# Sliding-window attention and a squared-ReLU feed-forward on one core: Strassen in seven up-projections instead of five, k and q of the short blocks in one transpose, and a scheduler's order shifted by fixed draws

## The chip, the cores and the metric

The kernel runs on one core of a Trainium2 chip. A core has five engines with a queue each: TensorE (PE, with its weight loads shown apart as PEld), VectorE (DVE), ScalarE (ACT), GpSimd (POOL) and SyncE (SP). Here PE does all matmuls and some transposes, DVE and ACT move and transform what PE leaves in its accumulation memory (PSUM, eight banks of 128 x 512 floats), POOL issues the input transfers, SP issues the output transfers and the transposes that the DMA engines do. The metric is the time on the device of one execution, in microseconds. The time before is the median of three runs, 292.88 (292.44 to 293.42).

## The reference

Eight batches, eight heads, 576 tokens, head size 64. Each token attends to itself and the 127 tokens before it, with a linear bias by distance whose slope depends on the head. The result, as 4608 tokens of 512 features, goes through a feed-forward of width 2048 with a squared ReLU.

```python
scores = scale * np.matmul(q, k.transpose(0, 1, 3, 2))
mask = (rel >= 0) & (rel < window)
scores = np.where(mask, scores + bias[None], -1000000000.0)
attn = np.exp(scores)  # after the row maximum is taken off
attn = attn / (np.sum(attn, axis=-1, keepdims=True) + 1e-09)
x = np.matmul(attn, v)              # then (batch, token, head*feature)
h = x @ w_in
r = np.maximum(h, 0.0)
return ((r * r) @ w_out).astype(np.float32)
```

## The kernel before

**Blocks and groups.** Attention works on blocks of tokens: each batch of 576 tokens is four blocks of 128 and a last one of 64, so there are 40 blocks (numbered m), eight of them short (m = 4, 9, 14, ...). The feed-forward works on nine groups of 512 tokens (g = 0 to 8), which do not line up with the blocks. Inputs are cast to bf16 as they are loaded; accumulation is in float32.

**Attention of a block.** `load_block` has POOL load k, q and v of a block (line 423). k and q lie one behind the other in a tile `kq` of 128 x 2 x 512. `prepare` turns them so that features lie on partitions, into `kqT`: blocks 0 to 10 by eight PE transposes of 128 x 128 (line 473) and a copy out of PSUM; from block 11 on (`KQ_DMA`) by one DMA transpose issued by SP (line 453). In a short block the transpose turns all 128 rows, though only 64 carry tokens. `scores` multiplies q with the keys of the block and of the one before it (lines 523 and 542; short blocks and first blocks of a batch use the second), ACT takes the exponential (line 581), and DVE multiplies with a mask that holds bias and window (line 592, tile `P`). `values` multiplies P with v and a column of ones (line 622), DVE takes reciprocals and normalises (lines 645 and 655) into `x`, and x is turned into `xT` (features on partitions) by PE (line 681) up to block 12 and by a DMA transpose (line 669) from block 13 on. `xT` is a ring of four groups.

**Up-projection.** A plain group (`fc_step`, line 728) takes, for each of 16 slices of 128 hidden features, four matmuls of 512 columns; ACT applies the ReLU (line 741), and DVE or ACT squares (lines 749 and 751) into `g`. A group in `FAST` takes Strassen's algorithm instead, in Winograd's form with seven products of half-size blocks: `token_sums` builds three sums and differences of the tokens' quarters on DVE (line 771), and four calls of `fast_unit` each run seven products of four matmuls of 256 columns (line 802) in three PSUM banks. Between the products ACT copies banks into SBUF (`fs`, `fu`, `fx`; lines 862, 883 and 872), DVE adds one back into a bank (line 868) and adds two others while it reads a bank (line 836). ReLU is on ACT (line 830) or on DVE or ACT (lines 841 and 843), squares on DVE or ACT (lines 851 and 853). `FAST` holds groups 4 to 8. The products of weights need sums of quarters of `w_in`, built once by DVE in `weight_sums` (line 386): sixteen steps of two instructions each.

**Down-projection.** Group 0 is plain (line 1036); groups 1 to 8 use Strassen (line 957), 112 matmuls of 256 columns each, with sums of `g` on DVE (line 916).

**Order.** All work is a list of tasks with a key, dependencies, buffers, and one duration for each engine that can do it. `Plan.order` walks a model of the chip ahead of the launch: at each step it gives the engine that can start first the ready task with the least key (within a wait of 100 ns on DVE and ACT), picks DVE or ACT where both are possible, and hands out PSUM banks. The resulting order of instructions is fixed on each engine; on the chip, semaphores enforce the dependencies. A stage of the feed-forward spans 128 units of the key: in stage g the up-projection of group g + 1 and the down-projection of group g are interleaved, and blocks of attention get due keys ahead of the group that needs them. The argument `shift` of `order` adds an offset to the key of each named set of tasks (same function, same rounded key); before the change nobody passes it. The DMA costs given to `load` are numbers for this model.

Of the kernel before, what the change touches and what calls it, by code (L numbers as in the profile page):

```python
# [10 lines left out]
AF = mybir.ActivationFunctionType  # L11
# [189 lines left out]
def kernel(  # L201
    ctx: ExitStack, tc: tile.TileContext, q, k, v, moe_w_in, moe_w_out, out
):
    nc = tc.nc

    B, H, S, D = q.shape
# [21 lines left out]
    SQUARES = 352.0  # L228
    FAST = range(NG - 5, NG)
    RING = 4 * 512  # L230
# [40 lines left out]
    def act(n):  # L271
        return n * 0.836 + 50.0

    def dve(n, rate=1):
        return n / rate / 0.96 + 68.0
# [116 lines left out]
    def load_block(m, key):  # L392
# [4 lines left out]
        for i, (nm, src) in enumerate((("k", k), ("q", q), ("v", v))):  # L397
# [26 lines left out]
            t_in[m, nm] = load(key + 0.01 * i, 920.0 if n == 128 else 600.0, emit, [t_ones] + (t_zeros if m >= NKB - 1 else []) if nm == "v" else [], [sl])  # L424

# [15 lines left out]
    def prepare(m):  # L441
# [9 lines left out]
        if kq_by_dma:  # L451
            def turn_kq():
                nc.sync.dma_start_transpose(kqT[sk.idx], kq[s_in[m, "k"].idx].rearrange("s t f -> s (t f)"))
            t_kq = [plan.add({"SP": 2000.0}, due - 80, turn_kq, [t_in[m, "k"], t_in[m, "q"]], [sk],
                             [s_in[m, "k"]], dma=900.0)]
        else:
# [3 lines left out]
            shared = Slot("t")  # L460
            for j, nm in ((j, nm) for hf in range(C // step) for j, nm in enumerate("kq")):
                hf = len(t_kq) // 2
# [3 lines left out]
                for i in range(hf * step, hf * step + step):  # L466
# [3 lines left out]
                    def emit(i=i, j=j, nm=nm, slot=slot, opens=fresh and i == hf * step, alloc=alloc):  # L470
                        if opens and slot.tile is None:
# [4 lines left out]
                    last = plan.add({"PE": mm(128)}, due - 56 + hf, emit,  # L476
                                    [last, t_ident, t_in[m, nm][hf] if m == 0 else t_in[m, nm]] + (chain["tp"] if opens else []),
                                    ([slot] if fresh and opens else []) + ([sk] if opens and not t_kq else []),
                                    [s_in[m, nm]] if j == 1 and i == C - 1 else [])
# [3 lines left out]
                if not apart and j == 0:  # L483
                    t_kq.append(None)
                    continue

                def evac(k=len(t_kq), j=j, slot=slot, lo=hf * step, hi=hf * step + step):
                    if apart:
                        copy(t_kq[k], kqT[sk.idx][:, j * C + lo:j * C + hi, 0:n],
                             slot.tile[:, j * 512:(j + 1) * 512].rearrange("p (c s) -> p c s", c=C)[:, lo:hi, 0:n])  # L490
                    else:
                        copy(t_kq[k], kqT[sk.idx][:, :, 0:n],
                             slot.tile.rearrange("p (c s) -> p c s", c=2 * C)[:, :, 0:n])
                w = step * n * (1 if apart else 2)
                t_kq.append(plan.add({"ACT": act(w), "DVE": dve(w, 2)}, due - 56 + hf, evac, [last], [], [slot]))
# [9 lines left out]
    def scores(ms):  # L505
# [20 lines left out]
        def burst(cs=range(C)):  # L526
# [4 lines left out]
            for m, sk, n, kb, parts, squares, slots, sE in todo:  # L531
                own, prev = kqT[sk.idx], kqT[sk_of[m - 1].idx] if kb else None
                for c in cs:
# [3 lines left out]
                    for i, (part, mk) in enumerate(() if squares else parts):  # L537
                        for half in range(2):
# [3 lines left out]
                            nc.tensor.matmul(sl.tile[:, at:at + n], kqT[sk_of[mk].idx][rows, c, :],  # L542
                                             own[rows, C + c, 0:n], start=True, stop=True)
        deps, acq, rel, cost = list(chain["s"]), [], [], 216.0
# [17 lines left out]
        for m, sk, n, kb, parts, squares, slots, sE in todo:  # L562
# [9 lines left out]
            for i, sl in enumerate(slots):  # L572
                w = one * H // len(slots)

                def expo(sl=sl, i=i, w=w, scores_e=scores_e, one=one, whole=len(slots) == 4):
                    if whole:
# [4 lines left out]
                    nc.scalar.activation(o, src, AF.Exp, bias=0.0, scale=scale)  # L581
                te = plan.add({"ACT": act(w)}, due - 28 + 3 * i, expo, [halves[i // 2 if m == 0 else 0]], [], [sl])
                if squares and i < 2:
# [110 lines left out]
    m = 0  # L694
# [385 lines left out]

    done = plan.order()
    kernel.plan = done
# [46 lines left out]
```

## Time and profile before

| what | us |
|---|---|
| median of three runs | 292.88 |
| the profiled execution's own time | 294.55 |
| span of the profiled execution, first to last instruction | 292.8 |
| TensorE busy | 281.9 (96% of the span) |
| DVE busy | 241.8 (83%) |
| ACT busy | 223.2 (76%) |
| POOL busy | 105.7 (36%) |

The granted TensorE clock is 0.999 over the span. Busy times are unions of the records of an engine: a record may begin before the one before it has ended, so the mean duration of one instruction times the count is more than the time that they keep the engine. PE's records are of modelled length, and a few are missing.

### The profile page before, as it was taken

What the parts mean: (1) busy time and instruction counts of PE and PEld (TensorE: products, weight loads), DVE (VectorE), ACT (ScalarE), POOL (GpSimd) and SP (SyncE); (2) the same over time, 40 slices, a digit from 0 to 9 for tenths busy, and PEclk for the clock granted to TensorE, in tenths of its full rate; (3) what the DMA queues carried; (4) which work ended last, traced back from release to release, by engine and by line L of the source; (5) the groups of instructions that cost most, each with busy time, mean ns of one, the idle gap of its engine ahead of it and who ended that gap; (6) DMA issues with size and microseconds to landing.
All of it is one profiled execution on the core that took longest, in us unless ns stands there. A gap on an engine that the chain in (4) does not pass through costs nothing.

```text
span 292.8 us, 9190 instructions
## 1 busy us (share of the span) xinstructions
PE 281.9 (96%) x3756; PEld 230.0 (79%) x3777; DVE 241.8 (83%) x584; ACT 223.2 (76%) x438; POOL 105.7 (36%) x131
## 2 busy tenths in 40 slices
PE   7799799999999999999999999999999999999995
PEld 6689678875666676666878888888888888888884
DVE  6948878695989856776989899999999997989833
ACT  6648868985578947779698989989989789578520
POOL 8937777651906443743623364332000000000000
PEclk9999999999999999999999999999999999999999
DMA  9999999999999999999999999999423111301223
GB/s 136 172 189 163 162 185 173 151 164 201 149 154 129 150 164 198 169 172 144 202 179 146 162 159 185 131 143 189 74 74 108 37 30 39 107 2 36 75 72 107
DMA packets 169946, 39.40 MB, mean 135 GB/s; under 512 B 157104, under 2 KB 169392, under 8 KB 169904
## 3 DMA queue, kind: packets, MB, share of 16 engines
q0 software_dynamic: 114656, 18.10, 92.9%
q1 hardware_dynamic: 54192, 20.46, 38.0%
q8 instruction: 29, 0.48, 0.7%
q10 hardware_dynamic: 1056, 0.26, 0.4%
q14 instruction: 13, 0.11, 0.1%
HBM read 36.70 MB, written 9.44 MB: 158 GB/s over the span
## 4 chain that ended last, share of the span: by engine, by line
PE 83%; DMA 6%; DVE 5%; ACT 3%; issue 2%; POOL 0%; ACTq 0%
PE o L957 32%; PE f L802 19%; PE h L728 16%; PE pv L622 6%; DMA w_in_sb<-in_moe_w_in_dram 5%; PE o L1036 4%; PE ps_s L523 3%; DMA raw<-in_q_dram 1%; PE ps_s L542 1%; PE tp L473 1%; DVE rt L836 1%; PE xp L681 1%; ACT rt L741 1%; DVE P L592 1%; DVE g L851 1%
## 5 line engine op out<-in xcount | busy, mean ns | idle before, releaser
L728 PE MATMUL h<-xT,w_in_sb 128*128 128x128 bf16 (+2 forms) x499 | 67.4, 270 | 3.5 <-issue 2.2
L581 ACT ACTIVATE E<-ps_s 128x384 bf16<-128x384 f32 (+2 forms) x130 | 58.5, 517 | 7.8 <-PE ps_s L523 7.5
L423 POOL DMA_DIRECT2D vt<-in_v_dram x40 | 34.2, 856 | 67.0 <-PE pv L622 57.1
L957 PEld LDWEIGHTS <-g 128*128 128x128 bf16 x512 | 49.1, 98 | 9.0
L592 DVE TENSOR_TENSOR P<-E,masks 128x1024 bf16<-128x1024 bf16 (+1 forms) x67 | 43.6, 661 | 11.1 <-ACT E L581 10.6
L741 ACT ACTIVATE rt<-h 128x512 bf16<-128x512 f32 x64 | 37.8, 603 | 19.1 <-PE h L728 16.8
L728 PEld LDWEIGHTS <-w_in_sb 128*128 128x128 bf16 x512 | 38.3, 98 | 11.8 <-issue 1.9
L423 POOL DMA_DIRECT2D kq<-in_k_dram x39 | 33.5, 860 | 25.0 <-DMA kqT<-kq 19.5
L957 PEld LDWEIGHTS <-S 128*128 128x128 bf16 x384 | 36.4, 98 | 6.7
L957 PE MATMUL o<-w_mix,S 128*128 128x256 bf16 x256 | 38.5, 273 | 0.0
L957 PE MATMUL o<-w_out_sb,g 128*128 128x256 bf16 x256 | 38.4, 273 | 0.0
L957 PE MATMUL o<-w_mix,g 128*128 128x256 bf16 x256 | 37.9, 273 | 0.0
L423 POOL DMA_DIRECT2D kq<-in_q_dram x39 | 33.5, 859 | 3.3 <-DMA w_in_sb<-in_moe_w_in_dram 1.8
L802 PEld LDWEIGHTS <-w_sum 128*128 128x128 bf16 x320 | 30.7, 98 | 4.3
L655 DVE TENSOR_TENSOR x<-pv,rec 128x256 bf16<-128x256 f32 (+1 forms) x80 | 32.9, 417 | 1.1
L622 PEld LDWEIGHTS <-P 128*128 128x128 bf16 x576 | 25.5, 97 | 8.2 <-DVE P L592 4.3
L622 PE MATMUL pv<-vt,P 128*128 128x65 bf16 x576 | 30.1, 193 | 1.7 <-DVE P L592 1.6
L830 ACT ACTIVATE rt<-f 128x512 bf16<-128x512 f32 x40 | 23.9, 597 | 8.2 <-PE f L802 6.7
L802 PE MATMUL f<-xT,w_in_sb 128*128 128x256 bf16 x160 | 26.1, 272 | 0.0
L802 PEld LDWEIGHTS <-w_in_sb 128*128 128x128 bf16 x240 | 23.1, 98 | 3.1
L853 ACT ACTIVATE g<-rt 128x512 bf16<-128x512 bf16 x39 | 24.5, 631 | 1.3 <-DVE rt L841 0.5
L802 PE MATMUL f<-T,w_sum 128*128 128x256 bf16 x160 | 24.5, 273 | 0.0
(78 smaller groups left out, 457.6 us busy)
## 6 DMA issues: line engine op xcount, KB each, us to landing
out_dram<-osb SPq DMA_DIRECT2D x35, 256.0 KB, 3.1
vt<-in_v_dram POOLq DMA_DIRECT2D x32, 128.0 KB, 6.3
kq<-in_k_dram POOLq DMA_DIRECT2D x31, 128.0 KB, 6.4
kq<-in_q_dram POOLq DMA_DIRECT2D x31, 128.0 KB, 6.7
w_in_sb<-in_moe_w_in_dram POOLq DMA_DIRECT2D x4, 512.0 KB, 10.3
w_out_sb<-in_moe_w_out_dram POOLq DMA_DIRECT2D x4, 512.0 KB, 8.9
kq<-in_k_dram POOLq DMA_DIRECT2D x8, 64.0 KB, 7.7
kq<-in_q_dram POOLq DMA_DIRECT2D x8, 64.0 KB, 7.8
```

What stands on the lines that cost most here:

```text
L423: nc.gpsimd.dma_start(o, src[b, :, kb * 128:kb * 128 + n, :].rearrange("h s d -> s h d"))
L581: nc.scalar.activation(o, src, AF.Exp, bias=0.0, scale=scale)
L592: nc.vector.tensor_tensor(Pt[sP.idx][:, hs, p0:2, 0:n], e, masks[:, hs, p0:2, 0:n], op=ALU.mult)
L622: nc.tensor.matmul(slot_v.tile[:, hi * (D + 1):(hi + 1) * (D + 1)], Pt[sP.idx][:, place(h), part, :], vt[s_in[mk, "v"].idx][:, h, :], star ...
L655: nc.vector.tensor_tensor(xt[sx.idx][0:n, hf * 256:(hf + 1) * 256].rearrange("p (h e) -> p h e", h=4), pv[0:n, :, 0:D], srec.tile[0:n, :]. ...
L728: nc.tensor.matmul(slot.tile[:, f * w:(f + 1) * w], w_in_sb[:, cc, (fc + f) * 128:(fc + f + 1) * 128], xT[:, cc, g * 512 % RING + lo:g * 5 ...
L741: nc.scalar.activation(srt.tile, slot.tile, AF.Relu, bias=0.0, scale=1.0)
L802: nc.tensor.matmul(bank[name].tile[:, jj * 256:jj * 256 + 256], w, m, start=opens and jj == 0 and k == 0, stop=k == 1, skip_group_check=True)
L830: nc.scalar.activation(srt.tile, bank[name].tile, AF.Relu, bias=0.0, scale=1.0)
L853: nc.scalar.activation(o, i, AF.Square)
L957: nc.tensor.matmul(bank[t].tile[:, t * 256:(t + 1) * 256], left(g, what, j)[:, t * 128:(t + 1) * 128], right(by, j), start=opens and j == ...
L1036: nc.tensor.matmul(bank.tile, g_slots[g].tile[:, fc, t * 128:(t + 1) * 128], w_out_sb[:, fc], start=fc == 0, stop=fc == FCB - 1)
```

## The change

1. `FAST` grows from the last five groups to the last seven: groups 2 and 3 are up-projected by Strassen too.
2. `weight_sums` is called in stage 1 instead of stage 2, and waits for the first matmuls of group 1 instead of those of group 2.
3. In a short block q is loaded into partitions 64 to 127 beside k (partitions 0 to 63) of the same 512 columns. One pass of four PE transposes, or a DMA transpose of half the columns, turns both; the scores then read q from columns 64 to 127 of `kqT`. The product with the block's own keys now has q's rows as well in its lower 64 partitions; the exponential therefore runs in two instructions, one on the 128 keys of the block before and one on the block's own 64 keys.
4. The model's load costs of short blocks change, and `order` gets offsets: nineteen seeded draws, each of which shifts a share of the named sets of tasks by up to 3, 8 or 16 units either way; tasks of the start-up (keys under -100000) are left out.

```diff
-    FAST = range(NG - 5, NG)
+    FAST = range(NG - 7, NG)
...
-            last = plan.add({"DVE": 2 * dve(256, 2)}, key, emit, [t_win[n], last, t_read[2][0]])
+            last = plan.add({"DVE": 2 * dve(256, 2)}, key, emit, [t_win[n], last, t_read[1][0]])
...
-                     else kq[sl.idx][0:n, i].rearrange("s (h d) -> s h d", h=H))
+                     else (kq[sl.idx][0:n, i] if n == 128 else kq[sl.idx][i * n:i * n + n, 0]).rearrange("s (h d) -> s h d", h=H))
...
-            t_in[m, nm] = load(key + 0.01 * i, 920.0 if n == 128 else 600.0, emit, ...)
+            t_in[m, nm] = load(key + 0.01 * i, 920.0 if n == 128 else {"k": 550.0, "q": 300.0, "v": 550.0}[nm], emit, ...)
...
-                nc.sync.dma_start_transpose(kqT[sk.idx], kq[s_in[m, "k"].idx].rearrange("s t f -> s (t f)"))
+                src = kq[s_in[m, "k"].idx]
+                if n == 128:
+                    nc.sync.dma_start_transpose(kqT[sk.idx], src.rearrange("s t f -> s (t f)"))
+                else:
+                    nc.sync.dma_start_transpose(kqT[sk.idx][:, 0:C], src[:, 0])
...
-            for j, nm in ((j, nm) for hf in range(C // step) for j, nm in enumerate("kq")):
+            for j, nm in ((j, nm) for hf in range(C // step) for j, nm in enumerate("kq" if n == 128 else "k")):
...
-                                             own[rows, C + c, 0:n], start=True, stop=True)
+                                             own[rows, C + c, 0:n] if n == 128 else own[rows, c, n:2 * n],
+                                             start=True, stop=True)
...
+                    if n < 128:
+                        o = scores_e().rearrange("p (a v x) (t q) -> p v t a x q", a=2, v=2, t=2)[:, i]
+                        src = sl.tile.rearrange("p (a x t q) -> p t a x q", a=2, x=2, t=2)
+                        for t, keys in enumerate((128, n)):
+                            nc.scalar.activation(o[0:keys, t], src[0:keys, t], AF.Exp, bias=0.0, scale=scale)
+                        return
...
-        if g == 2:
+        if g == 1:
             for n in range(4):
                 weight_sums(n, base + 64 * n)
...
-    done = plan.order()
+    SPREAD = ((195, 3, 1), (597, 3, 0.1), (1035, 3, 0.03), ...)
+    shift = dict.fromkeys(sorted({t.group for t in plan.tasks if t.group[1] > -100000}), 0.0)
+    for seed, most, share in SPREAD:
+        draw = random.Random(seed)
+        for group in shift:
+            if draw.random() < share:
+                shift[group] += draw.uniform(-most, most)
+    done = plan.order(shift)
```

More of the change, by code (lines that the diff above doesn't have):

```diff
@@ L1 @@
 import functools
+import random
 from contextlib import ExitStack
@@ L452, in turn_kq @@
             def turn_kq():
[L453 removed]
+                src = kq[s_in[m, "k"].idx]
[3 more added lines that the diff above has]
+                    nc.sync.dma_start_transpose(kqT[sk.idx][:, 0:C], src[:, 0])
             t_kq = [plan.add({"SP": 2000.0}, due - 80, turn_kq, [t_in[m, "k"], t_in[m, "q"]], [sk],
[L455 removed]
+                             [s_in[m, "k"]], dma=900.0 if n == 128 else 550.0)]
         else:
@@ L476, in prepare @@
                     last = plan.add({"PE": mm(128)}, due - 56 + hf, emit,
-                                    [last, t_ident, t_in[m, nm][hf] if m == 0 else t_in[m, nm]] + (chain["tp"] if opens else []),
+                                    [last, t_ident, t_in[m, nm][hf] if m == 0 else t_in[m, nm], None if n == 128 else t_in[m, "q"]] + (chain["tp"] if opens else []),
                                     ([slot] if fresh and opens else []) + ([sk] if opens and not t_kq else []),
-                                    [s_in[m, nm]] if j == 1 and i == C - 1 else [])
+                                    [s_in[m, nm]] if (j == 1 or n < 128) and i == C - 1 else [])
                     if fresh and opens:
@@ L482, in prepare @@
                 chain["tp"] = [last]
-                if not apart and j == 0:
+                if not apart and j == 0 and n == 128:
                     t_kq.append(None)
@@ L491, in evac @@
                     else:
-                        copy(t_kq[k], kqT[sk.idx][:, :, 0:n],
-                             slot.tile.rearrange("p (c s) -> p c s", c=2 * C)[:, :, 0:n])
-                w = step * n * (1 if apart else 2)
+                        cs = 2 * C if n == 128 else C
+                        copy(t_kq[k], kqT[sk.idx][:, 0:cs], slot.tile[:, 0:cs * 128].rearrange("p (c s) -> p c s", c=cs))
+                w = step * 128 * (1 if apart or n < 128 else 2)
                 t_kq.append(plan.add({"ACT": act(w), "DVE": dve(w, 2)}, due - 56 + hf, evac, [last], [], [slot]))
@@ L573, in scores, with expo @@
                 w = one * H // len(slots)
-                def expo(sl=sl, i=i, w=w, scores_e=scores_e, one=one, whole=len(slots) == 4):
+                def expo(sl=sl, i=i, w=w, scores_e=scores_e, one=one, whole=len(slots) == 4, n=n):
+                    if n < 128:
[4 more added lines that the diff above has]
+                        return
                     if whole:
@@ L581, in expo @@
                     nc.scalar.activation(o, src, AF.Exp, bias=0.0, scale=scale)
-                te = plan.add({"ACT": act(w)}, due - 28 + 3 * i, expo, [halves[i // 2 if m == 0 else 0]], [], [sl])
+                te = plan.add({"ACT": act(w) if n == 128 else 2 * act(w / 2)}, due - 28 + 3 * i, expo, [halves[i // 2 if m == 0 else 0]], [], [sl])
                 if squares and i < 2:
```

6 lines of the change are left out of this document (5 added, 1 removed).

## The prediction, written before the result was known

> **What bounds the kernel now.** I read the page's first part and its chain first, then busy time by stage, then the chain in order of time.
>
> ```profile
> span 292.8 us, 9190 instructions
> PE 281.9 (96%) x3756; PEld 230.0 (79%) x3777; DVE 241.8 (83%) x584; ACT 223.2 (76%) x438; POOL 105.7 (36%) x131
> ...
> PE 83%; DMA 6%; DVE 5%; ACT 3%; issue 2%; POOL 0%; ACTq 0%
> ```
>
> TensorE is busy for 96% of the span and is 83% of the chain that ended last. The stages say where the other 4% lie. The columns are the stretch in us, its length, then busy us (and instructions) of PE, PEld, DVE, ACT and POOL, the granted clock, DMA share and GB/s.
>
> ```profile
> 0.00:20.00 20.00, 16.51 (x288) 14.23 (x288) 14.25 (x46) 12.01 (x29) 14.53 (x22) 1.00 1.52 164
> 20.00:40.00 20.00, 18.06 (x387) 16.67 (x386) 14.87 (x37) 15.64 (x31) 14.88 (x18) 1.00 1.88 167
> 40.00:77.00 37.00, 36.31 (x527) 26.70 (x530) 29.56 (x77) 28.26 (x57) 22.22 (x27) 1.00 1.87 169
> 77.00:107.00 30.00, 29.47 (x363) 20.17 (x366) 24.28 (x77) 23.11 (x45) 14.23 (x17) 1.00 1.83 148
> 107.00:138.00 31.00, 30.52 (x385) 20.95 (x390) 22.36 (x52) 24.12 (x48) 13.40 (x17) 1.00 1.91 173
> 138.00:166.00 28.00, 27.65 (x373) 23.57 (x372) 25.77 (x58) 24.40 (x50) 12.30 (x15) 1.00 1.74 165
> 166.00:195.00 29.00, 29.00 (x414) 25.07 (x414) 28.15 (x67) 25.73 (x52) 12.35 (x15) 1.00 1.73 162
> 195.00:225.00 30.00, 30.00 (x425) 25.83 (x424) 29.20 (x68) 27.41 (x55) 1.80 (x3) 1.00 0.79 111
> 276.00:293.00 17.00, 13.34 (x123) 11.71 (x120) 6.97 (x13) 1.96 (x4) 0.00 (x0) 0.98 0.27 94
> ```
>
> Three kinds of stage are seen. Before 40 us PE idles 5.4 us. From 40 to 225 it idles about 2 us in 185, and part of that is matmul records that the trace lacks. From 166 to 225 it idles none. The last row holds the tail after the last matmul, about 3.5 us. So any TensorE time taken out behind 40 us shortens the run, as long as DVE and ACT keep up. The stretches 77:107 and 107:138 hold the plain up-projections of groups 2 and 3; 138 to 225 hold those of groups 4 to 6 by Strassen, where DVE already runs at 97% (28.15 of 29).
>
> What a matmul costs in a dense stream stands in the chain in order of time (start, us, what):
>
> ```profile
> 34.62 1.74 issue
> 89.86 0.86 PE h L728 x4
> 274.16 15.19 PE o L957 x139
> ```
>
> 139 matmuls of 256 columns in 15.19 us are 0.1093 each. Four of 512 columns in 0.86 are 0.215 each. Price follows columns. The first row is a PE pause of 1.74 us with no cause that the profile shows.
>
> The profiled execution took 294.55 us (span 292.8 and 1.75 around it), 1.67 above the median 292.88. That excess is about the size of the unexplained pause, which may be its own; I therefore work out the difference against 294.55 and carry it to the median.
>
> **Strassen for groups 2 and 3.** Each plain group is 64 matmuls of 512 columns: 64 x 0.215 = 13.76. By Strassen it is 4 units x 7 products x 4 = 112 of 256 columns: 112 x 0.1093 = 12.24. That is 1.52 less a group, 3.04 for two, all in a stretch where PE sets the time.
>
> A cross-check, by stages (stretch, length, DVE busy and count at the normalisations L655, clock, DMA):
>
> ```profile
> 107.00:138.00 31.00, 4.04 (x10) 1.00 1.91 173
> 166.00:195.00 29.00, 4.17 (x10) 1.00 1.73 162
> ```
>
> 107:138 (plain up, five blocks of attention by its ten normalisations) took 31 us, and 166:195 (Strassen, also ten) 29. The difference of 2.0 a group, 4.0 for two, is my far end; stage borders are rough, so I take 3.04.
>
> Behind the matmuls lie DVE and ACT. Rows of the five Strassen groups, and the plain relus of four:
>
> ```profile
> L741 ACT ACTIVATE rt<-h 128x512 bf16<-128x512 f32 x64 | 37.8, 603 | 19.1 <-PE h L728 16.8 <-DVE S L916 1.1 <-PE o L957 0.5
> L830 ACT ACTIVATE rt<-f 128x512 bf16<-128x512 f32 x40 | 23.9, 597 | 8.2 <-PE f L802 6.7 <-PE pv L622 0.8 <-DVE o L986 0.7
> L868 DVE TENSOR_TENSOR f<-f,fs 128x512 f32<-128x512 f32 x20 | 13.8, 692 | 0.3
> L836 DVE TENSOR_TENSOR rt<-f,fx 128x512 bf16<-128x512 f32 x20 | 13.7, 686 | 2.9 <-ACT fx L883 2.9
> L862 ACT ACTIVATE fs<-f 128x512 f32<-128x512 f32 x20 | 12.1, 603 | 2.5 <-PE f L802 2.4
> L841 DVE TENSOR_SCALAR rt<-rt 128x512 bf16<-128x512 bf16 x22 | 6.9, 315 | 0.6
> L843 ACT ACTIVATE rt<-rt 128x512 bf16<-128x512 bf16 x18 | 11.4, 632 | 1.5 <-DVE rt L836 1.2
> L771 DVE TENSOR_TENSOR T<-xT,T 128x512 bf16<-128x512 bf16 x10 | 4.1, 413 | 0.0
> ```
>
> Squares are 16 a group either way. A Strassen group adds on DVE four additions into PSUM (13.8 / 5 = 2.8), eight more out of it (2 x 13.7 / 5 = 5.5), the relus that DVE takes (6.9 / 5 = 1.4) and four token sums (4 x 0.413 = 1.7): 11.4. On ACT it swaps 16 relus (9.4) for 8 (23.9 / 5 = 4.8), 12 copies out of PSUM (3 x 12.1 / 5 = 7.3) and some relus (11.4 / 5 = 2.3): 5.0 more. These means overstate, because one starts before the last ends; the stages give the low bound: 28.15 - 22.36 = 5.8 on DVE and 25.73 - 24.12 = 1.6 on ACT.
>
> Is there room in 77:138? DVE idles 14.4 there and ACT 13.8. With the low bound DVE gains 11.6, loses the weight sums (below, 6.7), and the stage is 3 shorter: 6.5 are left idle. With the high bound 22.8 come and 6.7 go, 3 shorter: 4.7 too many, so squares must go to ACT, which has 13.8 - 10 - 3 = 0.8 left. Then 3.9 us of work over two engines have no place, 2.0 us of time. Between 0 and 2.0 I take 0.2, by the nearest row: three like stages (138 to 225) lost one wait of this kind, 0.35.
>
> ```profile
> 153.12 0.41 PE L622 MATMUL pv<-vt,P 128*128 128x65 bf16 x8 [0.35 <-DVE P L592]
> ```
>
> The token sums wait for the last turned block of their group, and behind them on DVE stand masks and normalisations, for which pv and the next blocks wait.
>
> ```profile
> L771 DVE TENSOR_TENSOR T<-xT x5: 417/418/419, 132.7 to 250.6; 128x512 bf16<-128x512 bf16 x5
> DMA to landing us min/median/max: 2.3/5.6/8.4
> ```
>
> ```profile
> 123.34 1.32 SPq L669 DMA_TRANSPOSE xT<-x  x1
> ```
>
> For group 4 the last turn is issued at 123.34 and lands by some 129 to 132; the sums start at 132.7, so they were not what DVE waited with. They delay each up-projection's start by some 1.7 us. What covers this is the down-projection of the group before: 112 matmuls, 12.2 us. Without the cover it costs 1.7 for each group.
>
> **Weight sums earlier.** 32 DVE instructions now run in 77:86 and will be free to run after the first matmuls of group 1, in 40:77 at the latest.
>
> ```profile
> 77.00:86.00 9.00, 6.71 (x32) 1.00 2.12 159
> ```
>
> DVE is busy with them for 6.7 (stretch, length, DVE at L386). It idles 7.4 in 40:77, so they just fit. Cost 0; if the cover is gone, masks and normalisations queue behind a pair of sums, 0.42 (6.71 / 16) each time.
>
> **k and q side by side.** Blocks 4 and 9 turn on PE with 4 transposes rather than 8.
>
> ```profile
> 38.21 0.39 PE L473 MATMUL tp<-ident,kq 128*128 128x128 bf16 x4
> ```
>
> ```profile
> L473 PE MATMUL tp<-ident,kq 128*128 128x128 bf16 x88 | 8.9, 225 | 0.4 <-DVE kq L437 0.3
> L437 DVE COPY kqT<-tp 128x1024 bf16<-128x1024 bf16 (+2 forms) x10 | 5.1, 513 | 1.3 <-PE tp L473 1.1
> L581 ACT ACTIVATE E<-ps_s 128x512 bf16<-128x512 f32 x30 | 15.9, 602 | 0.2 <-PE ps_s L542 0.2
> L581 ACT ACTIVATE E<-ps_s 128x256 bf16<-128x256 f32 x4 | 1.2, 396 | 0.0
> ```
>
> In the first row, of the order of time, four span 0.39 and one lasts 0.225, so they start 0.055 apart: 8 x 0.055 = 0.44. Block 4's lie ahead of 40 us, where PE idles anyway, so I take 0.3 (ends 0.2 and 0.44). The copy behind them halves, at two places, hidden. Six DMA transposes move half as much: PE waits for none, so 0. The exponentials of these eight blocks go from 16 of 512 elements to 32 of 256: at most 16 x (2 x 0.396 - 0.602) = 3.0 us more on ACT over the whole run; 0 on the path while ACT has 11% idle (25.73 of 29), and P of such a block 0.2 later if it has not. The transposes of k now wait for q too, which POOL issues right behind k; q's own transposes waited for it before, so the block is ready no later. The changed load costs are planner numbers and move no byte.
>
> **The fixed draws.** They shift priorities of everything but the loads, by a few units where a stage is 128. In 40 to 276 there is nothing to gain, for PE is full. Before 40 us 5.4 are idle; much of that waits for loads, which keep their places. From -2.0 (a third of that idle) to +1.0 (three waits like the one of 0.35), I take -0.2, near nothing, as most of the path lies where PE is full.
>
> **Sum.** -3.04 + 0.2 - 0.3 - 0.2 = -3.3. 294.55 becomes 291.2; the median 292.88 becomes 289.5.
>
> **A rule against it.** The Trainium skill, "TensorE: Matmul & The Clock Gate", section "Back-to-back issue gap", gives 131 ns a matmul of 512 columns and 81 of 128 in streams of weight loads and matmuls. An estimate between them is 98 for 256; a Strassen group would then take 112 x 0.098 = 11.0 against 64 x 0.131 = 8.4, and the change would lose 2.6 a group; the sum by it would be 292.9 + 5.2 - 0.3 = 297.8. The rows above, 0.215 and 0.109, disagree with both figures; the rival with the same sign is A.
>
> **Rivals.**
> A. *Price does not follow columns*: the weight load before each matmul sets the pace. Then 48 more loads a group cost 48 x 0.098 = 4.7, two groups 9.4: 302.3. For it: PEld is busy 25.07 of 29 in 166:195. Against: matmuls keep their 0.109 in such streams. Chance 0.02.
>
> ```profile
> L802 PEld LDWEIGHTS <-w_sum 128*128 128x128 bf16 x320 | 30.7, 98 | 4.3
> ```
>
> B. *DVE and ACT take half back*: the high bound of 2.0 holds in 77:138. 292.88 - 3.3 + 1.8 = 291.4. For it: DVE 97% in 166:195. Against: PE lost nothing there. Chance 0.17.
> C. *The tokens set the pace*: group 2's projection begins at 77.1, as soon as its last block is turned (the transposes at 76.15), so faster PE only waits. 292.88 - 0.3 = 292.6. Against: the down-projection of the group before is there to fill 12 us, and the end of the chain (15.19 us without a break) hangs on PE. Chance 0.06.
>
> ```profile
> 76.15 0.39 PE L681 MATMUL xp<-ident,x 128*128 128x128 bf16 x4
> 77.11 0.81 PE L728 MATMUL h<-xT,w_in_sb 128*128 128x512 bf16 x3
> ```
>
> D. *Slower*: orders are fixed ahead on each engine, so when DVE lags the plan, P comes late and pv holds PE, 0.35 each as at 153.12. From ten such waits on (3.3 / 0.35) the gain is gone; if each of the 11 blocks in 77:138 met it twice, 22 x 0.35 = 7.7 less 3.3: 297.3. Speaks for it: DVE full in five stages rather than three. Against: one such wait in three full stages. Chance 0.08.
> E. *The draws also close early gaps*: 2.0 instead of 0.2. 292.88 - 5.1 = 287.8. Chance 0.19.
>
> **Numbers.** My forecast, 289.5, has 0.48; its own range is 288.4 to 290.6. The range takes in E with the cross-check's larger gain, and B: 286.8 to 291.8. It leaves out C, D and A. About 0.3% (0.9 us) can be told from no change here: faster 0.84 (forecast, B, E), same 0.06 (C), slower 0.10 (D, A).
>
> **What would show it.** Up-projection matmuls: 128 of 512 columns gone, 224 of 256 more, still 0.109 apart. 80 transposes at L473 rather than 88. Weight sums before 77. DVE and ACT over 90% in 77:138 with PE idle under 1 us. The last 15 us run unchanged, some 3 us earlier. Wrong would be the forecast if PE shows waits for P, for f or for banks between 77 and 138, or if the idle before 40 changes by over 2 us.

## The result and the profile after

The changed kernel takes 291.67 us (median of 22 runs) against 293.53 for the kernel before on the same chip: a ratio of 0.9943, interval 0.9923 to 0.9964, or about 1.7 us. Ratios, here and below, leave out executions in a slower state (here one of the kernel before, 298.34), so they differ a little from the quotient of the medians. On the 292.88 of the prediction that ratio gives 291.2. The change makes the kernel faster, by about half of the 3.3 us forecast.

The profiled execution of the changed kernel took 291.83 us. Its page and its busy times by stage (columns as in the prediction):

```profile
span 290.0 us, 9439 instructions
PE 280.8 (97%) x3858; PEld 237.7 (82%) x3858; DVE 255.4 (88%) x626; ACT 228.5 (79%) x468; POOL 105.7 (36%) x131
...
PE 72%; DMA 11%; DVE 8%; POOL 4%; ACT 2%; issue 2%; POOLq 0%; ACTq 0%
```

```profile
0.00:20.00 20.00, 16.63 (x283) 14.00 (x283) 14.78 (x48) 12.04 (x28) 14.49 (x22) 1.00 1.53 165
20.00:40.00 20.00, 18.79 (x415) 16.96 (x415) 14.78 (x41) 16.57 (x34) 14.85 (x18) 1.00 1.83 166
40.00:77.00 37.00, 36.49 (x501) 26.38 (x500) 34.73 (x108) 29.20 (x60) 23.16 (x28) 1.00 2.02 165
77.00:107.00 30.00, 29.91 (x439) 25.25 (x437) 26.99 (x65) 25.75 (x56) 14.78 (x18) 1.00 2.17 167
107.00:138.00 31.00, 30.44 (x424) 25.64 (x423) 29.08 (x69) 25.24 (x54) 11.69 (x14) 1.00 1.61 166
```

DVE's busy time in 77:107 and 107:138 rose from 24.28 and 22.36 to 26.99 and 29.08, and of 40:77 from 29.56 to 34.73, where the weight sums now are. The share of PE in the chain fell from 83% to 72%. The chain says where. Its summary for 80 to 114 us, first before, then after (the second line is longer than is shown):

```profile
by line: PE h L728 43.2%; PE o L957 40.9%; PE pv L622 6.8%; PE ps_s L523 4.2%; PE ps_s L542 3.3%; issue 1.7%
```

```profile
by line: DVE P L604 14.3%; DVE x L667 12.0%; DVE rt L848 11.2%; DVE S L928 7.1%; issue 5.9%; ACT rt L842 4.9%; ACT fx L895 4.7%; DVE g L863 4.7%; PE f L814 4.3%; DVE rt L853 4.3%; PE o L969 4.3%; DVE g L928 3.7%; DVE o L998 3.6%; DVE osb L1
```

(Lines moved by 12: mask L592 is L604 after, normalisation L655 is L667, Strassen's product L802 is L814, down-projection L957 is L969.) Before, this stretch was TensorE but for 1.7% of issue. After, it runs through DVE's queue: masks, normalisations, reads of Strassen's banks, sums of `g`. The end of that stretch, in order of time, PE first, then DVE, then ACT (in brackets the idle time before, and who ended it):

```profile
111.69 0.43 PE L634 MATMUL pv<-vt,P 128*128 128x65 bf16 x8 [0.41 <-DVE P L604]
111.97 1.15 PE L969 MATMUL o<-w_out_sb,g 128*128 128x256 bf16 x9
113.26 0.49 PE L969 MATMUL o<-w_mix,g 128*128 128x256 bf16 x3 [0.15 <-ACT u L440]
```

```profile
108.45 0.65 DVE L928 TENSOR_TENSOR g<-g 128x1024 bf16<-128x1024 bf16 x1
109.03 0.41 DVE L667 TENSOR_TENSOR x<-pv,rec 64x256 bf16<-64x256 f32 x1
109.37 0.67 DVE L928 TENSOR_TENSOR S<-g,S 128x1024 bf16<-128x1024 bf16 x1
109.97 0.17 DVE L657 RECIPROCAL rec<-pv 64x4 f32<-64x4 f32 x1
110.06 0.65 DVE L1027 TENSOR_TENSOR osb<-o,u 128x512 f32<-128x512 f32 x1
110.64 0.40 DVE L667 TENSOR_TENSOR x<-pv,rec 64x256 bf16<-64x256 f32 x1
110.97 0.67 DVE L604 TENSOR_TENSOR P<-E,masks 128x1024 bf16<-128x1024 bf16 x1
```

```profile
106.81 1.06 ACT L593 ACTIVATE E<-ps_s 128x512 bf16<-128x512 f32 x2
112.62 0.60 ACT L440 ACTIVATE u<-o 128x512 f32<-128x512 f32 x1 [3.21 <-DVE o L998]
```

DVE has no gap in these rows. The exponentials that the mask at 110.97 reads had ended by 107.87, 3.1 us earlier, so the mask that PE waits for at 111.69 stood in line. The second pause, at 113.26, goes back to DVE as well: ACT's copy of `u` had waited for DVE's addition on L998.

**Measuring such pauses.** The table by stages understates them. A matmul of 256 columns is recorded as 0.273 us long while the next starts after 0.109, so PE looks busy through the first 0.16 us of a pause. I therefore took, from 76 us on, the distance from each PE start to the next, less the price of the first one's columns, and summed what exceeds 0.16. The changed kernel has five such pauses, 1.48 us together, between 87 and 150 us. The kernel before has one, 0.51 before `pv` at 153.12 (0.35 in its row); its trace lacks 21 matmul records, and the holes that they leave aren't counted.

The stretch in which these pauses lie can be timed by itself: from the last 512-column matmul of group 0's down-projection to the end of PE's work. Its ends in the two kernels (columns: count, durations, first to last start), before and then after:

```profile
L957 PE MATMUL o<-w_out_sb,S x128: 272/273/283, 104.1 to 289.1; 128*128 128x256 bf16 x128
L1036 PE MATMUL o<-w_out_sb,g x56: 377/379/390, 39.0 to 76.4; 128*128 128x512 bf16 x56
```

```profile
L969 PE MATMUL o<-w_out_sb,S x128: 272/273/283, 103.5 to 286.2; 128*128 128x256 bf16 x128
L1048 PE MATMUL o<-w_out_sb,g x64: 377/379/391, 37.8 to 75.8; 128*128 128x512 bf16 x64
```

Before it is 212.9 us, after 210.7. I call it the **rest**; it leaves out the loads of the first 76 us. The ledger closes: 212.9 less the one pause of 0.5, less 3.04 of columns, plus 1.48 of pauses is 210.8, and 210.7 was measured. The same sum for the experiments:

| kernel | PE pauses from 76 us, us | rest by the sum | rest measured |
|---|---|---|---|
| before's order, half loads | 0 | 212.4 | 212.5 |
| changed | 1.48 | 210.8 | 210.7 |
| changed, run again | 1.54 | 210.9 | 210.8 |
| changed, five more draws | 0.43 | 209.8 | 210.5 |
| changed, no draws | 4.17 | 213.5 | 213.8 |
| changed, no draws, relief | 2.80 | 212.2 | 212.0 |
| Strassen alone | 8.28 | 217.6 | 217.9 |
| Strassen alone, relief | 8.01 | 217.4 | 217.3 |

So the columns paid in all of them: the sums come within 0.3 us of the rest measured, with five more draws within 0.7. What differs is how long PE pauses.

### The profile page after: what moved, and what is told of

The parts are those of the page before. It is cut to its first block, busy times and chain, and to the rows that moved or that the text cites. A ratio compares the mean times of both kernels' runs of the same rounds, so it can differ in the third digit from the quotient of the medians.

```text
span 290.0 us, 9439 instructions
## 1 busy us (share of the span) xinstructions
PE 280.8 (97%) x3858; PEld 237.7 (82%) x3858; DVE 255.4 (88%) x626; ACT 228.5 (79%) x468; POOL 105.7 (36%) x131
## 4 chain that ended last, share of the span: by engine, by line
PE 72%; DMA 11%; DVE 8%; POOL 4%; ACT 2%; issue 2%; POOLq 0%; ACTq 0%
PE o L969 29%; PE f L814 27%; DMA w_in_sb<-in_moe_w_in_dram 5%; PE pv L634 4%; PE h L740 4%; DMA kq<-in_q_dram 4%; PE o L1048 3%; DMA w_out_sb<-in_moe_w_out_dram 2%; PE ps_s L528 2%; POOL kq L424 2%; DVE P L604 2%; POOL vt L424 1%; DVE x L667 1%; DVE rt L848 1%; PE ps_s L547 1%
## 5 line engine op out<-in xcount | busy, mean ns | idle before, releaser
L969 PEld LDWEIGHTS <-g 128*128 128x128 bf16 x512 | 48.7, 98 | 6.8 <-issue 0.3
L593 ACT ACTIVATE E<-ps_s 128x384 bf16<-128x384 f32 (+2 forms) x114 | 50.3, 508 | 4.2 <-PE ps_s L528 4.1
L814 PEld LDWEIGHTS <-w_sum 128*128 128x128 bf16 x448 | 42.9, 97 | 5.6
L604 DVE TENSOR_TENSOR P<-E,masks 128x1024 bf16<-128x1024 bf16 (+1 forms) x67 | 43.6, 659 | 0.8 <-ACT E L593 0.6
L842 ACT ACTIVATE rt<-f 128x512 bf16<-128x512 f32 x56 | 33.6, 603 | 8.5 <-PE f L814 7.3
L969 PEld LDWEIGHTS <-S 128*128 128x128 bf16 x384 | 36.5, 98 | 4.4
L969 PE MATMUL o<-w_mix,S 128*128 128x256 bf16 x256 | 38.1, 273 | 0.0
L969 PE MATMUL o<-w_mix,g 128*128 128x256 bf16 x256 | 37.3, 273 | 0.2 <-ACT u L440 0.2
L740 PE MATMUL h<-xT,w_in_sb 128*128 128x128 bf16 (+1 forms) x384 | 34.7, 237 | 2.3 <-DMA w_in_sb<-in_moe_w_in_dram 2.3
L969 PE MATMUL o<-w_out_sb,g 128*128 128x256 bf16 x256 | 36.7, 273 | 0.0
L814 PE MATMUL f<-xT,w_in_sb 128*128 128x256 bf16 x224 | 35.9, 273 | 0.0
L814 PEld LDWEIGHTS <-w_in_sb 128*128 128x128 bf16 x336 | 31.8, 97 | 4.8 <-DVE rt L848 0.3
L865 ACT ACTIVATE g<-rt 128x512 bf16<-128x512 bf16 x55 | 34.6, 639 | 0.8 <-DVE rt L853 0.2
L814 PE MATMUL f<-xT,w_sum 128*128 128x256 bf16 x224 | 33.7, 272 | 0.0
L667 DVE TENSOR_TENSOR x<-pv,rec 128x256 bf16<-128x256 f32 (+1 forms) x80 | 33.0, 415 | 0.4
L814 PE MATMUL f<-T,w_sum 128*128 128x256 bf16 x224 | 32.6, 273 | 0.0
L740 PEld LDWEIGHTS <-w_in_sb 128*128 128x128 bf16 x384 | 26.6, 98 | 4.7 <-DMA w_in_sb<-in_moe_w_in_dram 2.7
```

What stands on the lines that cost most here:

```text
L604: nc.vector.tensor_tensor(Pt[sP.idx][:, hs, p0:2, 0:n], e, masks[:, hs, p0:2, 0:n], op=ALU.mult)
L667: nc.vector.tensor_tensor(xt[sx.idx][0:n, hf * 256:(hf + 1) * 256].rearrange("p (h e) -> p h e", h=4), pv[0:n, :, 0:D], srec.tile[0:n, :]. ...
L740: nc.tensor.matmul(slot.tile[:, f * w:(f + 1) * w], w_in_sb[:, cc, (fc + f) * 128:(fc + f + 1) * 128], xT[:, cc, g * 512 % RING + lo:g * 5 ...
L814: nc.tensor.matmul(bank[name].tile[:, jj * 256:jj * 256 + 256], w, m, start=opens and jj == 0 and k == 0, stop=k == 1, skip_group_check=True)
L842: nc.scalar.activation(srt.tile, bank[name].tile, AF.Relu, bias=0.0, scale=1.0)
L865: nc.scalar.activation(o, i, AF.Square)
```

## The experiments

**One part undone or alone.** The first four runs take the change apart. Without the draws:

```diff
-    done = plan.order(shift)
+    done = plan.order()
```

> The changed kernel with the planner's order as before the draws (offsets all zero). Theory 1 (crowding: the two added Strassen groups fill DVE and ACT between 40 and 138 us, and PE waits there for about 1 us of the 3 gained): without the draws the waits are at best the same, so -1.7 us or less gain against the kernel before (-0.5 to -1.7). Theory 2 (front: the new order waits more for loads of weights and of k and q before 50 us, which eats 1 to 1.5 us): if the draws make that order, the gain grows to about -3. Theory 3 (tokens: a faster PE only waits for the next tokens): -1.7, no difference to the changed kernel.

294.96 against 293.95, ratio 1.0038 (1.0009 to 1.0067): a loss of 1.1 in place of the gain. Then five groups by Strassen with the rest of the change kept:

```diff
-    FAST = range(NG - 7, NG)
+    FAST = range(NG - 5, NG)
```

> The changed kernel with five Strassen groups as before; k and q side by side, early weight sums and draws stay. Theory 1: the two groups are worth 3.0 less 0.8 of crowding, so this is 2.2 slower than the changed kernel, +0.5 against the kernel before. Theory 2: the front keeps its loss of 1 to 1.5 and the 3.0 of Strassen are gone: +1.0 to +1.5. Theory 3: Strassen gave little, so this stays at -1 or better.

295.37, ratio 1.0049 (1.0012 to 1.0086): 1.4 slower than the kernel before. The draws alone on the kernel before (the nineteen of the change, passed to `order`):

> The kernel before with the draws as the only change. Theory 1: the draws have nothing to gain or to lose where PE is full, within 0.5 us of the kernel before. Theory 2: the draws disturb the front, +1.0 to +1.5. Theory 3: 0.

296.45, ratio 1.0094 (1.0061 to 1.0128): 2.8 slower. And Strassen alone, with the weight sums in stage 1, without side by side and draws:

```diff
-    FAST = range(NG - 5, NG)
+    FAST = range(NG - 7, NG)
...
-            last = plan.add({"DVE": 2 * dve(256, 2)}, key, emit, [t_win[n], last, t_read[2][0]])
+            last = plan.add({"DVE": 2 * dve(256, 2)}, key, emit, [t_win[n], last, t_read[1][0]])
...
-        if g == 2:
+        if g == 1:
```

> The kernel before with seven Strassen groups and the weight sums in stage 1, nothing else. By the sum of the prediction -2.8. Theory 1 (crowding): -1 to -2. Theory 4: -3.0 of matmuls and 2 to 3 of a new order, -1.0 to 0, or slower by what DVE and ACT add: up to +1.

299.86, ratio 1.0212 (1.0172 to 1.0252): 6.2 slower. Its waits of PE from 76 us on, in us, times and longest, and then those of the changed kernel without the draws (`fu` is written on line 872 of the kernel before and `fx` on 883, not the other way round; L874 after is L862 before, the copy `fs`):

```profile
PE f L802 <- ACT fu L872: 3.1, 4, 1.4
PE pv L622 <- ACT E L581: 1.0, 1, 1.0
PE pv L622 <- DVE P L592: 0.9, 2, 0.5
```

```profile
PE pv L634 <- DVE P L604: 0.8, 2, 0.5
PE o L969 <- ACT E L593: 0.5, 2, 0.3
PE f L814 <- ACT fs L874: 0.5, 1, 0.5
```

What follows: the parts don't add. Draws cost 2.8 on one program and save 2.8 on another (from +1.1 to -1.7). Each edit makes the planner place every task anew, and the order that results is worth up to several us either way.

**Other draws.** The same nineteen shares and sizes from other seeds (`random.Random(seed + 1)`):

> The changed kernel with other draws: each seed one higher, shares and sizes kept. Theory 4: an order that was not picked is 2 to 3 us slower than the changed kernel's, so +0.3 to +1.3 against the kernel before, like the run without draws. If spreading the keys helped by itself, as much as the draws on record: -1.7.

296.45, ratio 1.0103 (1.0072 to 1.0135). These lose 3.0. So the gain belongs to the draws that were chosen, not to spreading as such, as far as one other set shows it.

**Does less PE work buy time at all?** Here 16 matmuls of 512 columns are left out: in odd slices of groups 2 and 3 the up-projection adds three quarters of the features in place of four. First the planner knows of it:

```diff
+        depth = C - 1 if g in (2, 3) and fc % 2 else C
...
-            for cc in range(C):
+            for cc in range(depth):
```

> The kernel before with every second slice of the up-projections of groups 2 and 3 accumulated over three quarters of the features in place of four: 8 matmuls of 512 columns less in each group, 16 x 0.2158 = 3.4 us less of PE, and nothing more on DVE or ACT (these two groups' results are therefore left incomplete). Theory 1: the full saving comes out, -3.0 to -3.5. Theory 2: the same, since the front is that of the kernel before. Theory 3: less than -1, because the next tokens come no earlier.

293.88, ratio 0.9989 (0.9955 to 1.0023): nothing gained of 16 x 0.215 = 3.4. Then with the order of before kept, the tasks staying in place and emitting nothing:

```diff
+                    short = g in (2, 3) and fc % 2
+                    if short and cc == C - 1:
+                        return
```

> The kernel before in exactly its own order, with the same 16 matmuls of 512 columns in the up-projections of groups 2 and 3 not issued as in the run with fewer matmuls (those slices lack a quarter of the features); there the planner knew of the saving and made a new order, here it does not. Theory 4 (a new order costs: the order before is a picked one, and any change to the planner's input makes another that waits more, by 2 to 3 us): the saving comes out whole, -3.0 to -3.5. Theory 3 (tokens: loads and attention set the pace and a faster PE only waits): -1 to 0, as with the new order.

295.49, ratio 1.0075 (1.0038 to 1.0111): less work in the same order is slower by 2.0. The trace shows one place. A DMA transpose of `x` (chain, first fence) lands after 10.18 us; DVE stands at a token sum for it, the mask behind the sum is late (its exponentials had ended by 129.5), and PE waits for the mask:

```profile
121.52 10.18 DMA xT<-x
```

```profile
131.79 0.42 DVE L774 TENSOR_TENSOR T<-xT 128x512 bf16<-128x512 bf16 x1 [2.83 <-DMA xT<-x]
132.13 0.68 DVE L592 TENSOR_TENSOR P<-E,masks 128x1024 bf16<-128x1024 bf16 x1
```

```profile
132.87 0.41 PE L622 MATMUL pv<-vt,P 128*128 128x65 bf16 x8 [1.43 <-DVE P L592]
...
135.13 0.39 PE L542 MATMUL ps_s<-kqT 64*128 64x128 bf16 x4 [1.07 <-DVE g L752]
```

So in the old order a faster PE runs into its transfers. (The two pauses also halved the clock for 3.4 us; the last section has the rows.) The test is to halve k and q's loads from block 11 on (four heads of eight; the others keep what the buffer held), in before's order, without and with the skipped matmuls:

```diff
+                hs = slice(0, H if nm == "v" or m < KQ_DMA else H // 2)
+                nc.gpsimd.dma_start(o[:, hs], src[b, hs, kb * 128:kb * 128 + n, :].rearrange("h s d -> s h d"))
```

> The kernel before in exactly its own order, with k and q of blocks 11 to 39 loaded for four of the eight heads only (the other heads' features are what the buffer held, so the output is not the reference's): half of the input bytes of k and q there. Theory 3: the supply of tokens comes earlier and PE waits less, -1.0 or more. Theory 4: the supply is not what PE waits for, within 0.7 us of the kernel before.

> Both edits at once in the kernel before's own order: the 16 matmuls of groups 2 and 3 not issued, and k and q of blocks 11 to 39 loaded for four heads only (the output is left incomplete by both). Fewer matmuls alone came out 2.0 slower, half loads alone equal. Theory 3 (supply: PE gets ahead of the transposes that the DMA engines do, DVE stands at the token sums with the masks behind it, and PE waits for P): with the lighter input stream the transposes land in time and the saving of 3.4 comes out for the most part, -2 to -3.4. If something else in that order holds PE (the order itself): +1 to +2, as without the lighter loads.

Half loads alone: 293.43, ratio 1.0008 (0.9979 to 1.0038), no effect. With the skipped matmuls: 290.72, ratio 0.9894 (0.9858 to 0.9931), 3.1 of the 3.4. How long `kqT` takes to land, before, with skipped matmuls, and with skipped matmuls and half loads (least, median, most, us):

```profile
DMA to landing us min/median/max: 3.1/6.4/9.6
```

```profile
DMA to landing us min/median/max: 3.1/8.1/11.1
```

```profile
DMA to landing us min/median/max: 3.1/5.0/6.9
```

In before's order supply was a second limit just behind PE. Is it the changed kernel's?

> The changed kernel in its own order with k and q of blocks 11 to 39 loaded for four heads only (four heads' scores are not the reference's). Theory 3: the changed kernel too waits for the input stream, -0.7 or more against the changed kernel, so -2.4 or better against the kernel before. Theory 1 (crowding of DVE and ACT): no more than 0.4 better than the changed kernel, -1.5 to -2.1.

> Strassen for seven groups and early weight sums alone, in that kernel's own order (which was 6.2 us slower than the kernel before), with k and q of blocks 11 to 39 loaded for four heads only. If the input stream holds it: back by 3 us or more, +1 to +3 against the kernel before. If DVE and ACT hold it: +5 to +6, as before.

> The changed kernel without draws (1.1 us slower than the kernel before), in its own order, with the same half loads. If the draws do their work by fitting the input stream: back by 1.5 or more, -0.5 to -1.5 against the kernel before. If they fit DVE and ACT: +0.6 to +1.2.

The changed kernel with half loads takes 291.61, ratio 0.9921 (0.9894 to 0.9948), against 0.9943 without; Strassen alone with them 1.0192 (1.0156 to 1.0228) against 1.0212; no draws with them 1.0061 (1.0032 to 1.0090) against 1.0038. No: in all three the intervals overlap with those of full loads. Either these orders don't have that limit or it lies hidden behind another; the runs don't tell which.

**DVE and ACT.** If their work crowds, less of it must close the pauses. In the changed kernel's order the masks of blocks 13 to 23 were run over half the heads:

```diff
-                    hs = slice(lo, lo + step)
+                    hs = slice(lo, lo + (step // 2 if 12 < m_ < 24 else step))
```

> The changed kernel in its own order, with the mask multiplication of blocks 13 to 23 over half of the heads only (the other heads' P is left from an earlier block): about 11 x 2 x 0.3 = 6.6 us less of DVE between 77 and 138 us. Theory 1: DVE is what holds PE there, 0.5 to 1.0 better than the changed kernel, -2.2 to -2.7 against the kernel before. Theory 3 or neither: -1.5 to -1.9.

290.98, ratio 0.9897 (0.9860 to 0.9934). DVE's busy time in 77 to 138 fell by 2.3 us, the rest shrank from 210.7 to 210.2, the pauses from 1.48 to 1.07, and the wait of `pv` for P is no longer among PE's waits there, which fits; the intervals overlap, so by itself this only suggests it. A larger relief (masks, and the exponentials of blocks with four score banks, of blocks 13 to 29 over half the heads) on the two slower orders:

> The changed kernel without draws (+1.1 us), in its own order, with the same relief of DVE and ACT. Crowding: back by 1.5 or more, -0.5 to -2.0 against the kernel before. Otherwise +0.6 to +1.5.

> Strassen for seven groups and early weight sums alone, in that kernel's own order (6.2 us slower than the kernel before), with the mask multiplications of blocks 13 to 29 over half of the heads and the exponentials of their four-bank blocks over one head of two (the other heads' P and E are left from earlier blocks): some 9 us less of DVE and 6 to 9 of ACT between 77 and 170 us. Crowding of DVE and ACT: back by 3 us or more, +1 to +3 against the kernel before. If it is the order alone, through waits that no lighter engine shortens: +5 to +6.

Without draws, relief took the ratio from 1.0038 to 0.9974 (0.9947 to 1.0001), and pauses from 4.17 to 2.80: there, less work for DVE and ACT closes pauses, so crowding holds PE. That the draws mend the same pauses is likely, not shown. On Strassen alone it took 1.0212 to 1.0143 (1.0118 to 1.0167), but the profiled executions hardly differ (297.97 and 297.81), pauses fell only from 8.28 to 8.01, and the largest wait stays (lines moved by 2 there):

```profile
PE f L804 <- ACT fu L874: 3.4, 4, 1.6
```

This points to the place of Strassen's copies and additions in the queues as the limit there, more than to how much the engines have to do; no run moved them alone. How the remaining 8 us split over the chains behind `fu`, E and P isn't settled, nor where the medians differ by more than the profiles.

**Halved DMA transposes.** The changed order, but short blocks turned at full width:

> The changed kernel in its own order, but the six DMA transposes of short blocks turn both halves of the buffer as before (the second half is never read). If that halving matters to the input stream: 0.5 to 1.5 slower than the changed kernel. If, as forecast, it is worth nothing: within 0.3 of it.

> The changed kernel itself, on the same chip as the three others, for the comparison: -1.7 against the kernel before, by its interval -1.0 to -2.3.

291.89, ratio 0.9952 (0.9927 to 0.9977); the changed kernel again beside it 292.00, ratio 0.9938 (0.9907 to 0.9968). Halving them is worth nothing that can be measured.

**A version beyond both.** Five more draws on top of the nineteen:

```diff
-              (5619, 3, 0.1))
+              (5619, 3, 0.1), (1100312, 16, 0.03), (1100365, 16, 0.03), (1100516, 3, 0.03), (1101439, 16, 0.03),
+              (1101606, 6, 0.05))
```

> The changed kernel with five more draws behind the nineteen, picked by the length of the planner's own model. If the draws work by the model's account, a little faster than the changed kernel, -2.0 to -2.5 against the kernel before; if the model no longer tells orders apart at this size, -1.0 to -1.8.

291.26, ratio 0.9907 (0.9886 to 0.9929). It is clearly faster than the kernel before, and the fastest of all that compute the whole reference; its interval overlaps slightly with that of the changed kernel (0.9923 to 0.9964), so a lead of 1 us over it is likely rather than shown. In the two profiles the lead lies mostly ahead of the rest: its last 512-column matmul of group 0 starts at 74.2 against 75.8, while the rest is 210.5 against 210.7, though the pauses shrank from 1.48 to 0.43. Its stage 107:138:

```profile
107.00:138.00 31.00, 31.00 (x430) 26.56 (x427) 30.75 (x75) 25.49 (x54) 12.70 (x15) 1.00 1.80 172
```

DVE is busy for 30.75 of 31 us and PE for all 31. So a full DVE cost PE nothing here. What cost in the changed kernel was a queue in which the instruction that PE needed next stood behind others.

## Why the prediction came out as it did

The sign, the faster side and the range (286.8 to 291.8) held. The forecast, 289.5, did not: half of its gain came. The number that came, 291.2 on the same base, is nearly that of rival B (291.4), DVE and ACT taking half back, which had 0.17. It came only in part for B's reason: B put 2.0 on crowding, and 1.0 was measured.

**Right.** Price follows columns. The last row of the chain after holds 140 matmuls in 15.30, again 0.1093 each, and the sums in the table above close with 3.04 for two groups; with half loads in before's order, 16 skipped matmuls of 512 columns took 3.0 of 3.4 off the rest (212.5 to 209.5).

```profile
271.24 15.30 PE o L969 x140
```

Rival A is out, for the 256-column matmuls stay 0.109 apart. The figures of the Trainium skill that the prediction weighed ("TensorE: Matmul & The Clock Gate", section "Back-to-back issue gap") are out with it: by the estimate from them two more Strassen groups lose 5.2, and the same 0.109 stands against that. The transposes of k and q are 80 after, as worked out; halved DMA transposes are worth nothing; the weight sums fit into 40:77, with PE idle 0.5 there as before 0.7. The last 15 us are unchanged. Rival C, tokens, is not seen in the changed kernel.

**Wrong, first: the crowding term, 0.2.** I took 0.2 by the nearest row, one wait of 0.35. Measured from start to start, pauses went from 0.51 to 1.48, so the term is 1.0: PE saved 2.2 of 3.04 after 76 us. What the prediction had named as a sign against it, a wait for P between 77 and 138, is there, 0.41 at 111.69. DVE is at 90% and 94% of its two stages; ACT, at 86% and 81%, stayed under the 90% forecast. The row misled in two ways. It counts a pause only beyond 0.16, by the matmul's recorded length. And the three stages behind 138 were full but held an order with room for each late item; the new stages 77:138 didn't inherit that. Room on average (6.5 us by my low bound, 4.9 left idle as measured) isn't room in line: at 111.69 PE waited while DVE worked through the instructions that came first in its fixed order. The Trainium skill, "Perfetto Trace Analysis", section "Tensor Engine Instruction (MATMUL, LD_WEIGHTS)", notes that ACT and DVE are strict FIFO. The rows of DVE from 108.45 to 110.97 agree: the mask starts only when all before it have.

**Wrong, second: 0.5 ahead of 76 us.** Transposes (-0.3) and draws (-0.2) were to come off the front. The last 512-column matmul of group 0 starts at 76.4 before and 75.8 after, which looks like it; but in other runs of before's order it lies between 75.1 and 76.7, and of the changed order between 75.4 and 76.9. Nothing can be claimed. The largest wait of PE there in the changed kernel is for a load of weights:

```profile
PE h L740 <- DMA w_in_sb<-in_moe_w_in_dram: 2.3, 2, 1.2
```

It is 0.5 in the profile before, but 1.8 in before's order with half loads, so it can't be put down to the change either. With 1.0 for crowding and nothing ahead of 76 us, the sum gives 3.04 - 1.0 = 2.0. The interval of the ratio, 1.1 to 2.3 us, holds that.

**Not a term, but a trap: the two profiles.** 294.55 and 291.83 differ by 2.72, which looks like most of the forecast. The first holds the unexplained pause of 1.74 and lies 1.0 above the median of its 22 runs; the second lies 0.16 above its own. What is left is the 1.9 that the medians differ by. The prediction took the pause as perhaps the run's own: three other profiles in before's order hold no unexplained pause over 1.0.

**Wrong in its ground: the draws at -0.2 as an edit of their own.** I costed each edit as if the rest of the order stood still. Strassen with side by side but no draws is +1.1, not -3.1; the draws are -2.8, not -0.2. The two errors, 4.2 and 2.6, cancelled in large part, and the 1.6 that is left is the whole miss: that the sign and the range held is luck to that extent. Rival D described what happens without them, P late and `pv` held (0.8 us in the rows without draws), plus what no rival named: PE waiting for Strassen's own copies, 3.1 us at `fu` in Strassen alone. Its 0.08 was for the changed kernel, where it didn't come true; but it was the draws that kept it away, and I had given them next to nothing. Rival E, draws closing early gaps, named 2.0 where 2.8 came, at the wrong place: the rest shrank from 213.8 to 210.7 by the draws, on pauses that the kernel before doesn't have, and the part ahead of it didn't shrink (75.2 and 75.8).

Open: which tasks the draws moved that matter. The traces show that pauses went from 4.17 to 1.48, not which of the shifts did it.

## What to carry to other kernels

Where a planner or a fixed order sets the queues, an edit is priced in two parts: its work, and the new order. The second can be larger than the first and has either sign; an edit of 3 us of PE work came out between +6.2 and -2.7 us here. To price the first alone, keep the order and leave the work out; if that gains nothing, look for a second limit just behind the engine you relieve. And count pauses on PE from start to start: the recorded length of a 256-column matmul hides the first 0.16 us of each.

## What the runs showed of the hardware

**Two microseconds of pause in one slice of 3.41 us halve the clock of the next.** With skipped matmuls and full loads, PE paused for 1.59 and 1.23 us (from start to start) ahead of 132.87 and 135.13. Four stretches of that kernel, the granted clock behind ACT's and POOL's columns:

```profile
133.00:134.00 1.00, 1.00 (x27) 0.61 (x25) 1.00 (x5) 0.46 (x1) 0.11 (x1) 1.00 2.33 44
134.00:135.00 1.00, 0.06 (x4) 0.00 (x0) 0.97 (x4) 1.00 (x3) 0.77 (x1) 0.75 1.29 123
135.00:136.00 1.00, 0.87 (x10) 0.62 (x11) 0.80 (x2) 0.42 (x2) 0.38 (x1) 0.50 1.95 154
136.00:138.00 2.00, 2.00 (x9) 0.96 (x8) 0.00 (x0) 0.37 (x1) 0.99 (x2) 0.52 2.20 156
```

The rows fit a clock of 0.5 from 134.5 to 137.9, which costs about 1.4 us more (half of the 0.87 and 2.0 us in which PE was busy from 135 on). Three other profiles hold such a drop in the midst of the work, each 3.41 us long: the other draws (after pauses of 1.68 and 0.73), full transposes, and five groups, there after a single long pause of 2.1 us:

```profile
34.43:37.85 3.42, 1.50 (x49) 1.26 (x49) 3.27 (x9) 2.57 (x7) 1.56 (x3) 1.00 1.97 171
37.85:41.26 3.41, 3.41 (x40) 3.41 (x38) 0.60 (x2) 1.55 (x3) 1.86 (x3) 0.50 1.91 173
```

All four drops begin a whole number of steps of 3.413 us after the clock of that run first went to full. Cut so, the slices just ahead of the drops hold 2.2 to 2.3 us of idle PE (the slice less the price of its columns). The idlest slices at full clock without a drop behind them, in all twenty profiles, hold 2.0; one of them has most of the 1.74 of the kernel before. Where the pauses fall matters too: in Strassen alone 3.41 us from 155.7 on hold 2.3 of idle PE (pauses of 0.51 and 1.58 and smaller ones), but two slices share them, and the clock stayed at 1.00. The Trainium skill, "TensorE: Matmul & The Clock Gate", section "What's actually happening", puts the drop to half at one idle window or more of about 3.4 us. The length fits, but here the window was never idle throughout: two thirds of it sufficed. So a wait of a microsecond and a half can cost twice itself, if another falls into the same slice. The bound between 2.0 and 2.2 us is read from four drops only.

**A DMA transpose landed later the more was loaded beside it.** In before's order the same transposes of k and q landed after 6.4 us at the median with full loads and 4.2 with half loads; where PE ran ahead with the skipped matmuls, after 8.1 (11.1 at most) and 5.0.
